# Four tiles instead of two for the decoded weights on their way to DRAM, two of them in the last operand of the attention

## The chip, the cores and the metric

The kernel runs on one core of one Trainium2 chip. The metric is the device time of one execution in microseconds (us), lower is better; the time given for a kernel is the median of its runs.

## The reference, cut to what matters

The program is an attention layer followed by two feed-forward layers, in float32 precision (every matrix product below is built from two parts of each operand, a high and a low one).

```python
# attention, per batch and head (4 x 8 heads, 576 rows, width 64)
scores = (q @ k.T) / 8 + minimum(-(cum_t - cum_s), 0), causal   # cum: running sum of max(s, 0)
x = softmax(scores) @ v                       # -> (4, 576, 512)
# first layer, per batch
h = maximum(x @ w_in, 0); u, v = h[..., :512], h[..., 512:]
v_s = w_spatial @ layernorm(v) + b_spatial
x = (u * v_s) @ w_out
# second layer
x_prev = x shifted by one row
xk = mu_k * x + (1 - mu_k) * x_prev;  xr = mu_r * x + (1 - mu_r) * x_prev
out = sigmoid(xr @ w_r) * (maximum(xk @ w_k, 0) ** 2 @ w_v)
```

All inputs arrive as 64-bit floats. The weight matrices are decoded in the kernel: each 128x256 block of 64-bit values becomes a float32 high part and a float32 low part.

## The kernel before, in words

**Decoding the weights.** The six weight matrices (`d_wv`, `d_wu` from `moe_w_in`, `d_wo`, `d_wk0`, `d_wk1`, `d_wr`, `d_w2`; lines 203 to 208) are cut into 64 jobs of 128x256 values. A job goes through five parts (lines 118 to 154):

- `dL` (line 120): a DMA on SyncE's (SP's) queue loads 256 KB into a tile `raw`, of which there are three (pool `stl`).
- `dF` (lines 128, 129): two ScalarE (ACT) instructions make `g` and a scaled low word from it.
- `dD` (lines 134, 136, 139): three VectorE (DVE) instructions, then one addition on GpSimd (POOL, line 141), give the float `f`.
- `dT` (lines 146 to 150): ACT copies `f`, rounded, into the first half of a tile `hl` (line 101), and POOL subtracts that from `f` into the second half (line 116). The pool `stg` gives two tiles `hl`, used in turn.
- `dS` (line 153): a DMA on SP's queue stores `hl` (256 KB) into the DRAM tensor of its matrix.

Each part takes the oldest job that the part before it has finished. `dec_step` (line 164) issues one of each, in the order `dS dT dD dF dL`, so a job moves on by one part per step and a load is used by `dF` two steps after it. Line numbers such as L101, L116 are those of shared helpers: on ACT L101 is only this copy; on POOL and DVE L116 is any two-part subtraction, told apart by the tile it writes.

**Order.** Nothing is scheduled by the compiler: every engine and the SP queue run their instructions in the order in which the program issues them. Up to the end of the attention, written-out lists (`START`, `ORDER`, `TAIL1`, `TAIL2`, lines 526 to 595 and 866 to 870) say where each decode part stands among the other work. After `TAIL2` comes the loop over the four batches `b` (lines 893 to 938). For each: `gate_u` (8 units, for b > 0, a decode step after every second one), `spatial` (8 units, a step after every second), `gate_v` of the next batch (4 or 5 units of 12 matmuls, a step after every second), `proj` (8 units, a step after every second). All these matmuls go to eight PSUM tiles used in turn. `tick()` (line 641) issues what was put off from the unit before.

**What gate_v needs.** During the first four `spatial` units the next batch's activations are split (`split_x`, lines 658 to 667): ACT copies the high part `XH` (line 659), and one tick later DVE subtracts it (L116, `big<-x`) to give the low part `XL`. Each `gate_v` unit begins with matmuls over `XH` and `XL` of parts 0 to 3 in this order (`three`, line 676; L682 in the profile).

**BIG.** The tile `BIG` (line 72) holds three groups of 5,120 float32 per partition. In the attention a group holds the four operands U, W, V, X of a pair of heads. Pair 15, the last one, uses group 0. After it, columns 0 to 4095 of group 0 hold the weight `WU`; group 1 holds `XH` and `XL`, group 2 the weight `WV`. Columns 4096 to 5119 of group 0, the end of X of pair 15, are used by nothing in the kernel before. The last matmuls that read X of pair 15 are those of `st_E(15)` (L440), issued in `TAIL1`.

Of the kernel before, what the change touches and what calls it, by code (L numbers as in the profile page):

```python
# [9 lines left out]
F32R = mybir.dt.float32r  # L10
# [15 lines left out]
def tile_kernel(  # L26
# [47 lines left out]
    def part_of(g, c0, n, w):  # L74
        return BIG[:, g].rearrange("p a b -> p (a b)")[:, c0:c0 + n * w].rearrange("p (n w) -> p n w", n=n)
# [7 lines left out]
    rctx = ctx.enter_context(ExitStack())  # L83

    def pool(c, name, bufs, space=None, **kw):
        if space is not None:
            kw["space"] = space
        return c.enter_context(tc.tile_pool(name=name, bufs=bufs, **kw))

    wdram = pool(rctx, "wdram", 1, bass.MemoryType.DRAM)  # L90
    stg = pool(rctx, "stg", 2, side="right")
    stl = pool(rctx, "stl", 3, side="right")
    WN = 256
    jobs, loaded, first = [], [], []
    n_done, last = [0], {}

# [18 lines left out]
    def subtract(eng, **kw):  # L115
        (nc.gpsimd if eng == "P" else nc.vector).tensor_tensor(op=ALU.subtract, **kw)  # L116

    def dec_load(j):
        t = stl.tile([128, WN], I64, tag="raw", name="raw")
        nc.sync.dma_start(out=t, in_=j[0])  # L120
        loaded.append((t,) + j[1:])

    def dec_first(t, *dst):
        w32 = t.bitcast(I32).rearrange("p (n t) -> p n t", t=2)
        low = t.bitcast(U32).rearrange("p (n t) -> p n t", t=2)[:, :, 0]
        top, topf = w32[:, :, 1], t.bitcast(F32).rearrange("p (n t) -> p n t", t=2)[:, :, 1]
        g = stg.tile([128, WN], F32, tag="g", name="g")
        nc.scalar.activation(out=g, in_=topf, func=ACTF.Abs)
# [3 lines left out]
    def dec_second(low, top, g, *dst):  # L132
# [4 lines left out]
            out=gi, in0=gi, scalar1=3, scalar2=0x3FFFFFFF, op0=ALU.logical_shift_left, op1=ALU.bitwise_and)  # L137
        f = stg.tile([128, WN], I32, tag="f", name="f")
        nc.vector.scalar_tensor_tensor(  # L139
# [4 lines left out]
    second, third = [], []  # L144

    def dec_third(f, dst):
        hl = stg.tile([128, 2, WN], F32R, tag="hl", name="hl")
        COPY[ENGINE["dH"]](hl[:, 0, :], f.bitcast(F32))
        subtract(ENGINE["dO"], out=hl[:, 1, :], in0=f.bitcast(F32), in1=hl[:, 0, :].bitcast(F32))
        third.append((hl, dst))  # L150

    def dec_store(hl, dst):
        nc.sync.dma_start(out=dst, in_=hl.bitcast(F32))
        n_done[0] += 1

    PARTS = {"dS": (third, dec_store, 0), "dT": (second, dec_third, 0), "dD": (first, dec_second, 0),
             "dF": (loaded, dec_first, 1), "dL": (jobs, lambda *j: dec_load(j), 0)}

# [10 lines left out]
    def weight(nm, src, c0, n):  # L169

        d = wdram.tile([128, 2, n, 512], F32, name=nm)
        for kc in range(n):
            for o in range(0, 512, WN):
                jobs.append((src[128 * kc:128 * kc + 128, c0 + o:c0 + o + WN], d[:, :, kc, o:o + WN]))
        last[nm] = len(jobs)
# [633 lines left out]
    def prep_b():  # L809
        b_lo = WS[1][96:97, 4, :]  # L810
        nc.scalar.copy(WS[1][64:65, 4, :], brow[64:65, :])
        nc.scalar.copy(b_lo, brow[96:97, :])
        nc.vector.tensor_tensor(out=b_lo, in0=brow[96:97, :], in1=b_lo.bitcast(F32), op=ALU.subtract)
# [69 lines left out]
    def prep_0():  # L883
        nc.gpsimd.memset(WS[1][64:128, 4, :].bitcast(F32), 0.0)
        prep_b()

    tail["B0"] = prep_0
    for nm in TAIL2.split():
        tail[nm]()
# [165 lines left out]
```

## Time and profile before

| | |
|---|---|
| three runs | 707.02, 708.51, 709.27 us (median 708.51) |
| the profiled execution | 707.71 us |
| its span, first to last instruction | 706.0 us |
| mean granted TensorE clock | 0.995 |
| busy: TensorE (PE), DVE, ACT, POOL | 677.7, 507.0, 374.3, 355.1 us |

The profile is one execution. Times of rows are us from the start of its span. PE is TensorE's matmuls, PEld its weight loads, SPq an instruction in SyncE's queue. In a timeline row, the text in brackets is how long the engine sat idle before that instruction and what ended the idle time. PEclk is the granted TensorE clock, 1.00 being 2.4 GHz and 0.50 being 1.2 GHz.

### The profile page before, as it was taken

How to read it: one execution, taken by the hardware profiler on the slowest of the kernel's cores; microseconds unless marked ns; L12 is line 12 of the kernel's file. 1: busy time of each engine (PE TensorE's matmuls, PEld its weight loads, DVE VectorE, ACT ScalarE, POOL GpSimd, SP SyncE). 2: the span in 40 equal slices, each digit the busy share in tenths (PEclk: the TensorE clock that was granted, in tenths of full speed). 3: DMA queues.
4: the chain of work that ended last, by engine and by line, in shares of the span. 5: the costliest groups of instructions: out<-in, count | busy, mean ns of one | idle time of the engine just before them, and what ended most of it. 6: DMA issues, size and time to landing. Idle time of an engine off the chain costs nothing.

```text
span 706.0 us, 11479 instructions
## 1 busy us (share of the span) xinstructions
PE 677.7 (96%) x3842; PEld 596.2 (84%) x3842; DVE 507.0 (72%) x1054; ACT 374.3 (53%) x840; POOL 355.1 (50%) x528
## 2 busy tenths in 40 slices
PE   4899999999999989999998999999999999999998
PEld 3687777778877789999998899998989889898987
DVE  8867677767762578857867858369788786968763
ACT  6678988989983475554555535341332414133230
POOL 4635656656566557446646637442434434244430
PEclk9999999999999999999999999999999999999999
DMA  8344645555447627454244466360001010000101
GB/s 180 95 107 126 163 120 154 134 138 151 118 112 233 210 84 220 135 170 129 93 144 154 141 210 205 107 285 16 31 0 46 1 45 2 16 31 0 45 1 45
DMA packets 100930, 77.61 MB, mean 110 GB/s; under 512 B 66949, under 2 KB 83749, under 8 KB 100359
## 3 DMA queue, kind: packets, MB, share of 16 engines
q1 hardware_dynamic: 98455, 76.28, 36.6%
q10 hardware_dynamic: 2416, 0.60, 0.4%
q8 instruction: 30, 0.49, 0.3%
q14 instruction: 29, 0.24, 0.1%
HBM read 54.05 MB, written 21.79 MB: 107 GB/s over the span
## 4 chain that ended last, share of the span: by engine, by line
PE 64%; DVE 10%; DMA 9%; ACT 8%; issue 3%; POOL 3%; SPq 2%; ACTq 0%; DVEq 0%; POOLq 0%
PE mm L682 43%; PE mm L767 5%; PE ps L440 4%; PE pv L487 4%; PE s L401 3%; DMA q<-in_q_dram 3%; DMA rd<-r 2%; ACT big L364 2%; PE pv L484 2%; PE t L347 2%; DMA r<-pt 2%; DMA d_wr<-hl 1%; DMA d_w<-hl 1%; DVE jk L408 1%; DVE big L369 1%
## 5 line engine op out<-in xcount | busy, mean ns | idle before, releaser
L682 PE MATMUL mm<-big 128*128 128x384 f32 (+2 forms) x1176 | 208.4, 336 | 6.3 <-ACT vr L719 3.0
L682 PEld LDWEIGHTS mm<-big 128*128 128x128 f32 x1176 | 193.7, 190 | 17.7 <-DVE big L116 4.0
L408 DVE CUSTOM_DVE_ANT_0 jk<-s,mask 128x288 bf16<-128x288 f32 (+4 forms) x160 | 64.3, 429 | 36.4 <-PE s L401 35.5
L682 PE MATMUL mm<-w,vb 128*128 128x512 f32 (+1 forms) x304 | 90.4, 381 | 0.0
L972 DVE TENSOR_TENSOR r<-r 128x384 f32<-128x384 f32 x48 | 53.7, 1119 | 46.6 <-ACT r L969 46.6
L440 PE MATMUL ps<-big 128*128 128x288 f32 (+4 forms) x384 | 84.5, 336 | 0.6
L401 PE MATMUL s<-big 128*128 128x448 f32 (+3 forms) x192 | 74.0, 427 | 7.7 <-DVE mx L408 3.6
L116 POOL TENSOR_TENSOR hl<-f,hl 128x256 fp32r<-128x256 f32 x64 | 50.6, 791 | 55.4 <-ACT hl L101 49.8
L460 ACT ACTIVATE e<-ps 128x288 f32<-128x288 f32 (+3 forms) x160 | 64.8, 435 | 21.7 <-PE ps L440 19.1
L141 POOL TENSOR_TENSOR f<-f,raw 128x256 int32<-128x256 int32 x64 | 51.6, 806 | 49.0 <-DVE f L139 23.0
L487 PE MATMUL pv<-e,vp 128*128 128x448 f32 (+3 forms) x256 | 73.7, 387 | 0.0
L440 PEld LDWEIGHTS ps<-big 128*128 128x128 f32 x384 | 61.7, 199 | 13.9 <-issue 7.2
L682 PEld LDWEIGHTS mm<-w,vb 128*128 128x128 f32 x304 | 56.0, 188 | 11.2
L401 PEld LDWEIGHTS s<-big 128*128 128x128 f32 x192 | 37.9, 206 | 30.1 <-DVE mx L408 23.8
L992 DVE RECIPROCAL rr<-rr 128x512 f32<-128x512 f32 x18 | 60.4, 3353 | 0.6
L515 POOL TENSOR_TENSOR x<-pt,rb 64x576 f32<-64x576 f32 x32 | 45.4, 1420 | 26.3 <-DMA rb<-rd 23.3
L464 POOL TENSOR_SCALAR_AFFINE_SELECT e<-e 128x128 f32<-128x128 f32 (+1 forms) x160 | 41.8, 287 | 30.0 <-ACT e L460 28.9
L767 PE MATMUL mm<-ws,vb 128*128 128x288 f32 x384 | 56.1, 295 | 0.0
L973 ACT CAST vb<-r 128x384 fp32r<-128x384 f32 x48 | 24.6, 513 | 56.9 <-DVE r L972 56.9
L767 PEld LDWEIGHTS mm<-ws,vb 128*128 128x128 f32 x384 | 52.6, 188 | 0.0
L682 PE MATMUL mm<-gh,wo 128*128 128x288 f32 x256 | 51.4, 295 | 0.0
L708 POOL TENSOR_TENSOR gh<-mix,vb 128x384 fp32r<-128x384 f32 x24 | 25.4, 1069 | 49.2 <-ACT vb L707 49.2
(129 smaller groups left out, 1329.6 us busy)
## 6 DMA issues: line engine op xcount, KB each, us to landing
rb<-rd SPq DMA_DIRECT2D x16, 288.0 KB
out_dram<-rr SPq DMA_DIRECT2D x17, 256.0 KB
q<-in_q_dram SPq DMA_DIRECT2D x32, 128.0 KB
raw<-in_moe_w_in_dram SPq DMA_DIRECT2D x16, 256.0 KB
vp<-in_v_dram SPq DMA_DIRECT2D x32, 128.0 KB
raw<-in_moe_w_k_dram SPq DMA_DIRECT2D x16, 256.0 KB
d_wk<-hl SPq DMA_DIRECT2D x16, 256.0 KB
raw<-in_moe_w_v_dram SPq DMA_DIRECT2D x16, 256.0 KB
```

The lines of the kernel that those rows point to most:

```text
L116: (nc.gpsimd if eng == "P" else nc.vector).tensor_tensor(op=ALU.subtract, **kw)
L141: nc.gpsimd.tensor_tensor(out=f, in0=f, in1=low, op=ALU.add)
L401: nc.tensor.matmul(out=ps[:, 0:kn], lhsT=W[g][:, h, 128 * i:128 * i + 128], rhs=X[g][:, h, k0:k0 + kn], start=True, stop=True,)
L408: nc.vector.tensor_tensor_reduce(out=jk[r0:128, 0:kn], in0=ps[r0:128, 0:kn], in1=mask[r0:128, m0:m0 + kn], scale=1.0, scalar=(dst if mid e ...
L440: nc.tensor.matmul(out=ps[:, o:o + b - a], lhsT=st[g][:, h, 128 * j:128 * j + 128], rhs=mv[g][:, h, 64 + a:64 + b], start=(n == 0), stop=( ...
L460: nc.scalar.activation(out=e[:, o:o + n], in_=ps[:, 0:n], func=ACTF.Exp)
L487: nc.tensor.matmul(out=pv[:, 1, 448 - w:448], lhsT=lt, rhs=e[:, OFF[j]:OFF[j] + w], start=False, stop=(j == 4),)
L515: (nc.gpsimd if ENGINE[f"n3{h}"] == "P" else nc.vector).tensor_tensor(out=X1[64 * h:64 * h + 64, hp, b, 1:S + 1], in0=hold["t"][0:64, h, : ...
L682: nc.tensor.matmul(out=ps, lhsT=x, rhs=y, start=(m == 0), stop=(m == n - 1))
L767: nc.tensor.matmul(out=o, lhsT=x[:, sc, dd], rhs=y[:, sc, t], start=(sc == 0 and m == 0), stop=False)
L972: nc.vector.tensor_tensor(out=r, in0=r, in1=r, op=ALU.mult)
L992: nc.vector.reciprocal(out=r, in_=r)
```

## The change

The two tiles `hl` are taken out of the pool `stg` and made two tiles of a pool of their own, kept in a list `ring` and used in turn. Before `TAIL2` two more tiles are appended to the list: views of columns 4096 to 4607 and 4608 to 5119 of group 0 of `BIG`. From there on four tiles are used in turn.

```diff
     stg = pool(rctx, "stg", 2, side="right")
     stl = pool(rctx, "stl", 3, side="right")
+    sth = pool(rctx, "sth", 1, side="right")
     WN = 256
+
+    ring = [sth.tile([128, 2, WN], F32R, name=f"hl{i}") for i in range(2)]
...
     def dec_third(f, dst):
-        hl = stg.tile([128, 2, WN], F32R, tag="hl", name="hl")
+        hl = ring.pop(0)
+        ring.append(hl)
         COPY[ENGINE["dH"]](hl[:, 0, :], f.bitcast(F32))
         subtract(ENGINE["dO"], out=hl[:, 1, :], in0=f.bitcast(F32), in1=hl[:, 0, :].bitcast(F32))
         third.append((hl, dst))
...
+    ring.extend(part_of(0, 4096 + 512 * i, 2, WN) for i in range(2))
     tail["B0"] = prep_0
     for nm in TAIL2.split():
         tail[nm]()
```

## Rows read from the trace of the kernel before

**Rows 1.** The page, part 1: busy us, share, instructions of TensorE.

```profile
PE 677.7 (96%) x3842; PEld 596.2 (84%) x3842; DVE 507.0 (72%) x1054; ACT 374.3 (53%) x840; POOL 355.1 (50%) x528
```

**Rows 2.** Waits of PE, 235 to 445 us, complete: us in total, times, longest.

```profile
PE mm L682 <- ACT vr L719: 3.0, 1, 3.0
PE mm L682 <- DVE big L116: 2.6, 3, 2.0
PE mm L682 <- ACT x L785: 0.4, 1, 0.4
PE mm L792 <- ACT ut L758: 0.2, 1, 0.2
```

**Rows 3.** Timeline of PE: gate_v of batches 1, 2, 3 (start, us, matmuls).

```profile
278.17 11.09 PE L682 MATMUL mm<-big 128*128 128x512 f32 x48
...
329.32 2.72 PE L682 MATMUL mm<-big 128*128 128x512 f32 x11
332.35 11.40 PE L682 MATMUL mm<-big 128*128 128x512 f32 x49 [0.31 <-DVE big L116]
...
383.81 2.02 PE L682 MATMUL mm<-big 128*128 128x512 f32 x8
...
387.79 0.96 PE L682 MATMUL mm<-big 128*128 128x512 f32 x3 [1.96 <-DVE big L116]
...
389.06 10.28 PE L682 MATMUL mm<-big 128*128 128x512 f32 x37 [0.32 <-DVE big L116]
```

**Rows 4.** Windows, PE alone: length, busy us (matmuls), PEclk, DMA share, GB/s.

```profile
390.00:391.00 1.00, 1.00 (x4) 0.50 0.09 30
```

**Rows 5.** Timeline of DVE: three of batch 3's four XL subtractions.

```profile
380.79 0.74 DVE L116 TENSOR_TENSOR big<-x,big 128x576 fp32r<-128x576 f32 x1
...
386.59 1.14 DVE L116 TENSOR_TENSOR big<-x,big 128x576 fp32r<-128x576 f32 x1
...
388.02 0.99 DVE L116 TENSOR_TENSOR big<-x,big 128x576 fp32r<-128x576 f32 x1
```

**Rows 6.** Waits of ACT, whole span, those on the stores of `hl`.

```profile
ACT hl L101 <- DMA d_wk<-hl: 15.4, 9, 2.9
...
ACT hl L101 <- DMA d_w<-hl: 12.8, 6, 5.8
...
ACT hl L101 <- DMA d_wr<-hl: 7.9, 6, 2.6
```

**Rows 7.** Timeline of ACT: copies into `hl`, the first two are seven steps apart.

```profile
359.55 0.41 ACT L101 CAST hl<-f 128x256 fp32r<-128x256 f32 x1 [1.54 <-POOL f L141]
...
380.80 0.41 ACT L101 CAST hl<-f 128x256 fp32r<-128x256 f32 x1 [1.42 <-DMA d_w<-hl]
...
416.54 0.41 ACT L101 CAST hl<-f 128x256 fp32r<-128x256 f32 x1 [5.79 <-DMA d_w<-hl]
```

**Rows 8.** The chain that ended last, 361 to 372 us: start, us, what.

```profile
361.99 4.04 DMA d_wr<-hl
...
366.61 0.74 POOL hl L116
367.34 0.76 POOL f L141
...
368.12 0.34 SPq L120
...
368.55 2.88 DMA d_wr<-hl
```

**Rows 9.** Timeline of DVE: one step's part of the decoding.

```profile
369.95 0.60 DVE L134 TENSOR_SCALAR g<-g 128x256 f32<-128x256 f32 x1 [1.19 <-ACT g L128]
370.59 0.73 DVE L136 TENSOR_SCALAR g<-g 128x256 int32<-128x256 int32 x1
371.41 0.43 DVE L139 SCALAR_TENSOR_TENSOR f<-raw,g 128x256 int32<-128x256 int32 x1
```

**Rows 10.** Instructions on the tile `hl`, 250 to 440 us: count, duration ns, starts.

```profile
L101 ACT CAST hl<-f x44: 399/407/412, 257.2 to 432.9; 128x256 fp32r<-128x256 f32 x44
```

## The prediction

> **What bounds the kernel now.** I read the page's busy times first: TensorE is busy for 677.7 of the 706.0 us [rows 1]. Where one engine is that full, only its holes can be won, so the next view is the list of PE's waits over the stretch in which the four tiles exist, from the start of `TAIL2` to the end of the decoding. It is short and complete [rows 2]: 3.0 us on ACT's line 719, 2.6 us on DVE's line 116, 0.4 us on ACT's line 785, 0.2 us on ACT's line 758. The wait on line 719 ends before the first copy into `hl` that `TAIL2` issues (257.2 us, [rows 10]), since it belongs to the last `gate_v` units of batch 0 that `TAIL1` issues. The change can't reach it. The other three can be reached.
>
> The timeline of PE places the 2.6 us [rows 3]. They lie in `gate_v`: 0.31 us at 332 us and 1.96 and 0.32 us at 388 and 389 us, each time on a subtraction `big<-x`, which is `XL`. So PE has run out of everything else and waits for the low part of the next batch's activations. The hole costs more than its idle time: the same 48 matmuls take 11.09 us in `gate_v` of batch 1 and, for batch 3, run from 383.81 to 389.06 + 10.28 = 399.34 us, which is 15.53 us. The difference is 4.44 us, of which 2.28 are idle. The other 2.16 us are the clock: after the hole the granted clock is 0.50, that is 1.2 GHz, where it was 2.4 GHz [rows 4].
>
> Why is `XL` late? The waits of ACT say it: before the copy into `hl` ACT waits 15.4 + 12.8 + 7.9 = 36.1 us, 21 times, for the stores of `hl` [rows 6]. ACT runs in order, so its copy of `XH` (line 659) stands behind those waits, and DVE's `XL` behind `XH`. The chain view shows the loop that sets this pace [rows 8]: POOL finishes a tile and the addition behind it (0.74 and 0.76 us), that frees a `raw` tile, SP issues the load it had been stuck on (0.34 us), and only then the store that stands behind the load; the store takes 2.88 or 4.04 us, and ACT may then write that tile again. With two tiles this loop closes every second step.
>
> **The change part by part.** *Tiles of their own in place of the pool's two, before `TAIL2`.* The same two tiles, in the same order, as many instructions; the copy still waits for the store of two steps earlier. None of the waits in rows 6 lies in the attention's stores (`d_wv`, `d_wu`), so nothing is hidden there that could appear. Zero; its cover is that no instruction is added. Should the tracked waits differ by a semaphore instruction, I bound that at some hundredths of a us, each way, beside other work.
>
> *Two more tiles from `TAIL2` on.* No DMA, ACT or POOL instruction is added or moved; 44 copies [rows 10] go to four tiles in place of two. Their first use has to wait for the last reader of X of pair 15, a matmul that `TAIL1` issued long before. From then on a copy waits for the store of four steps earlier, issued three steps before. A store in the loop above lands within two steps, so these waits should go.
>
> *What is late next.* With the stores gone, the decoding's next loop is that of the three `raw` tiles, closed every third step: SP's issue 0.34 us, the load's landing, an ACT pass of about 0.41 us, DVE's three (0.60 + 0.73 + 0.43 = 1.76 us, [rows 9]), POOL's addition 0.76 us. The landing of a load has no row here; the nearest rows are the stores of the same 256 KB, 2.88 and 4.04 us, and I keep both ends. That is 6.2 to 7.3 us for three steps, 2.1 to 2.4 us a step. Now a step takes (380.80 - 359.55) / 7 = 3.04 us [rows 7]. Over those seven steps ACT gains 4.2 to 6.8 us, so `XH` and `XL` of batch 3 come earlier by that much, as far as PE's own `spatial` results allow.
>
> *What is enough.* PE needs the third `XL` at 383.81 + 2.02 = 385.83 us and gets it at 386.59 + 1.14 = 387.73; it needs the fourth three matmuls later (3 x 11.09 / 48 = 0.69 us), at 386.5, and gets it at 388.02 + 0.99 = 389.01 [rows 3, 5]. So 2.5 us earlier closes the hole, and the slower end of the estimate gives 4.2. At 2.7 us a step it would just be closed. The same holds one batch before, where the hole is 0.31 us and ACT waits for `d_wk` even longer.
>
> *The sum.* Batch 3's `gate_v`: 4.44 us, idle and clock. Batch 2's `gate_v`: from 329.32 to 343.75 is 14.43 us for 60 matmuls, against 60 x 11.09 / 48 = 13.86, so 0.57 us [rows 3]. The wait on line 785: 0.38 us at most; it is a copy of `proj` that stood behind ACT's longest wait on a store, 5.79 us [rows 7], and that goes too: 0.4 us. Line 758's 0.2 us lies in `TAIL2` before any wait on a store; nothing. Together 5.4 us. After 440 us the decoding is over and PE has no hole until the last units of the output, so what is won is kept: every fetch of a weight stands behind PE's own reading of the buffer and moves with it. The profiled execution takes 707.71 us, its span and 1.7 around it; less 5.4 that is 702.3. The median of the runs shown is 0.8 above that execution, so the forecast is 703.1 us.
>
> **The rivals.** *The loads take the stores' place.* If a load landed only after some 5 us, the loop over `raw` would take 8.3 us for three steps, 2.8 a step, and ACT would wait on line 128 as it now does on line 101. For it: SP issues load and store back to back, and faster steps put more of them on the queues. Against it: the two landings shown are below that. The hole of batch 3 would shrink by perhaps half a microsecond and the clock would fall all the same: 708 us. Chance 0.11.
>
> *DVE and POOL get in each other's way.* The same subtraction `XL` takes 0.74, 1.14 and 0.99 us [rows 5], longer where POOL is at work. If ACT's waits had been keeping the two apart, DVE would now lose that on most of its work, 0.4 us on each operation with two operands in SBUF. Some six of these stand between the first `spatial` result and the fourth `XL`, so 2.4 us would come off the 4.2 to 6.8 gained, at the lower end 1.8 would be left of the 2.5 needed, and a hole of 0.7 us with the fall of the clock behind it would cost 0.7 + 2.16 = 2.9 of the 4.44: 706.0 us. Against it: most of that stretch already runs at the longer times. Chance 0.06. The Trainium skill, "SBUF — State Buffer", section "Who interferes with whom", speaks for this rival: it says that a DVE instruction with two SBUF inputs contends with a GpSimd instruction that reads SBUF, and that the loser is blocked for the whole instruction. By that rule alone a blocked `XL` could lose up to a POOL pass, 0.74 us, and the trace's 0.25 to 0.40 agrees in direction.
>
> *Slower: the new tiles are taken for the whole of BIG.* If the waits were derived for `BIG` as one object, each matmul that reads any of it would wait for the last write into the two new tiles. Half of the 44 steps write there; PE would wait for at least the copy and the subtraction, 0.41 + 0.74 us, 22 times: 25 us more, 734 us. It decides from the first step that writes such a tile with PE behind it. Against it: DVE's and ACT's writes of `XL` and of `mix`, and the fetches into WU and WV, go into other parts of `BIG` beside matmuls that read it, and PE's complete list of waits names no transfer [rows 2]. Chance 0.05.
>
> *It doesn't do what it says* would be four tiles whose waits stay, since a store is issued late rather than landing late. But SP lets one store pass per step, so never more than two are open; it would look like the first rival, 708 us, and is in its chance.
>
> **How the numbers follow.** Forecast 0.78, loads 0.11, contention 0.06, slower 0.05. A measurement of this kernel tells about 0.3%, 2.1 us, from no change: faster is below 706.4. The forecast's own range is 701.5 (the runs shown reach 1.5 below their median) to 704.7 (the holes of batch 2 and line 785 stay, and 0.6 of the rest). To hold the time 8 times in 10 the range goes on to 706.9, over the contention case; no change and slower are left out. Faster: the forecast and part of the contention case, 0.80. Same: the rest of it and the loads, 0.15. Slower 0.05.
>
> **What would show it right or wrong.** Right: no wait of ACT's line 101 on a store after 257 us, or a few tenths in all; what is left there is on POOL's line 141; PE without idle between 320 and 440 us of its span, clock 1.00 throughout; the 48 matmuls of batch 3's `gate_v` in 11.1 us; the 3.0 us on line 719 unchanged. Wrong: ACT waiting for `raw` at line 128; `XL` still ending later than PE needs it; any wait of PE on `hl`; or a new hole after 440 us that gives the gain back.

## The result: 6.2 us faster, and the profile after

| | before, on the same chip | after |
|---|---|---|
| median (range) | 707.76 us (706.56 to 709.27), 4 runs | 701.29 us (700.02 to 701.61), 4 runs |
| ratio after/before, 95% interval | | 0.9912 [0.9893, 0.9931] |
| the profiled execution, its span | 707.71, 706.0 us | 700.02, 698.3 us |

The ratio is worked out from all the runs of both kernels and is not the quotient of the two medians; it is 6.2 us of 707.76, between 4.9 and 7.6. The forecast was 5.4 us and 703.1 us: faster, as predicted. The median is 1.8 us below the forecast and 0.2 us below 701.5, the low edge of its range. Part of that is the kernel before, which ran faster here than in the three runs that the forecast started from: set against their 708.51 us the ratio gives 0.9912 x 708.51 = 702.3 us, inside the range. In the lines of the changed kernel most numbers are three to five higher: L101, L116, L120, L141 are now L104, L119, L123, L144, and L682, L719, L758, L785 are now L686, L723, L762, L789. Half of the decoded tiles lie in `BIG`, so a tile `hl` shows as `big` in two steps of four.

Part 1 of the page of the changed kernel, beside [rows 1]: PE is busy 5.1 us less with the same 3842 matmuls.

```profile
PE 672.6 (96%) x3842; PEld 592.2 (85%) x3842; DVE 497.9 (71%) x1054; ACT 376.8 (54%) x840; POOL 355.8 (51%) x528
```

The waits of PE from 235 to 445 us, complete, beside [rows 2]. Nothing of the wait on DVE's subtraction and nothing of the wait on the copy of `proj` is left. The wait on line 723 stands (2.6 for 3.0 us). The waits on line 762 have grown from 0.2 to 1.3 us; the section on the hardware says where they come from.

```profile
PE mm L686 <- ACT vr L723: 2.6, 1, 2.6
PE mm L686 <- ACT ut L762: 1.1, 2, 0.9
PE mm L796 <- ACT ut L762: 0.2, 1, 0.2
```

The timeline of PE in the changed kernel: `gate_v` of batches 1, 2 and 3, beside [rows 3], and last the `gate_u` of batch 3. Each is one stretch without a bracket, that is without idle time. Batch 3's 48 matmuls take 11.09 us as batch 1's do, where they took 15.53; batch 2's 60 take 13.81 in place of 14.43.

```profile
276.52 11.09 PE L686 MATMUL mm<-big 128*128 128x512 f32 x48
...
327.67 13.81 PE L686 MATMUL mm<-big 128*128 128x512 f32 x60
...
381.54 11.09 PE L686 MATMUL mm<-big 128*128 128x512 f32 x48
...
405.12 12.88 PE L686 MATMUL mm<-big 128*128 128x288 f32 x96
```

The waits of ACT in the changed kernel, 245 to 440 us, beside [rows 6]: 36.1 us on stores are gone without a rest, and over the whole span too no copy waits for a store. What ACT now waits for in the decoding is POOL's addition and the loads: 6.7 + 5.0 + 1.4 = 13.1 us on `raw`.

```profile
ACT g L131 <- DMA raw<-in_moe_w_v_dram: 6.7, 4, 2.9
ACT g L131 <- DMA raw<-in_moe_w_k_dram: 5.0, 5, 2.6
ACT hl L104 <- POOL f L144: 4.7, 6, 1.3
...
ACT big L104 <- POOL f L144: 3.4, 5, 1.5
...
ACT g L131 <- DMA raw<-in_moe_w_r_dram: 1.4, 2, 0.9
```

The timeline of ACT in the changed kernel, copies of steps one, six and eight of the same stretch as [rows 7]. From the first to the sixth are five steps in 11.79 us, 2.36 us each; all seven take 370.14 - 352.27 = 17.87 us, 2.55 each, where [rows 7] had 21.25 and 3.04. The last two steps are slower, 3.04 us each: by then ACT has caught up and waits for PE's results (1.19 us on line 762 ahead of the seventh copy).

```profile
352.27 0.41 ACT L104 CAST big<-f 128x256 fp32r<-128x256 f32 x1 [1.53 <-POOL f L144]
...
364.06 0.41 ACT L104 CAST hl<-f 128x256 fp32r<-128x256 f32 x1
...
370.14 0.40 ACT L104 CAST big<-f 128x256 fp32r<-128x256 f32 x1
```

**Where the time went.** The last long piece of the chain of waits gives a mark behind the decoding. In the changed kernel it is the following line, and it ends at 695.08 us, 313.54 us after batch 3's `gate_v` began.

```profile
432.84 262.24 PE mm L686 x1344
```

In the kernel before the same piece ends at 702.80, 318.99 us after that `gate_v` began at 383.81: 5.45 us were lost behind that point. With the 0.62 of batch 2's `gate_v` it is 6.07 us. The two spans differ by 7.7. The other 1.6 us lie before the two added tiles can act: the hole on line 719 began at 246.07 us before and on line 723 at 244.73 after, and part of the difference is the price of that hole. That this part varies from execution to execution is shown by other executions: in experiment 2, with the same attention, this hole ends at 252.36 us, in the changed kernel at 247.36, and in the kernel before at 249.03 in the one profile and 247.22 in the other.

### The profile page after: what moved, and what is told of

Read it like the earlier page. It is cut to its first block, busy times and chain, and to the rows that moved or that the text cites. A ratio compares the mean times of both kernels' runs of the same rounds, so it can differ in the third digit from the quotient of the medians.

```text
span 698.3 us, 11475 instructions
## 1 busy us (share of the span) xinstructions
PE 672.6 (96%) x3842; PEld 592.2 (85%) x3842; DVE 497.9 (71%) x1054; ACT 376.8 (54%) x840; POOL 355.8 (51%) x528
## 4 chain that ended last, share of the span: by engine, by line
PE 76%; DMA 7%; ACT 6%; DVE 4%; SPq 2%; issue 2%; POOL 1%; ACTq 0%; DVEq 0%; POOLq 0%
PE mm L686 54%; PE mm L771 7%; PE ps L444 3%; PE pv L491 3%; DMA q<-in_q_dram 3%; PE s L405 2%; DMA rd<-r 2%; ACT big L368 2%; PE pv L488 2%; PE t L351 2%; DVE jk L412 1%; DMA r<-pt 1%; SPq L256 1%; DVE big L373 1%; ACT e L464 1%
## 5 line engine op out<-in xcount | busy, mean ns | idle before, releaser
L686 PE MATMUL mm<-big 128*128 128x384 f32 (+2 forms) x1176 | 204.3, 332 | 3.8 <-ACT vr L723 2.6
L686 PEld LDWEIGHTS mm<-big 128*128 128x128 f32 x1176 | 191.4, 188 | 13.3 <-ACT vr L723 2.9
L686 PE MATMUL mm<-w,vb 128*128 128x512 f32 (+1 forms) x304 | 90.4, 381 | 0.0
L144 POOL TENSOR_TENSOR f<-f,raw 128x256 int32<-128x256 int32 x64 | 51.8, 809 | 48.6 <-DVE f L142 22.7
L444 PEld LDWEIGHTS ps<-big 128*128 128x128 f32 x384 | 60.1, 194 | 14.5 <-issue 7.4
L686 PEld LDWEIGHTS mm<-w,vb 128*128 128x128 f32 x304 | 56.0, 188 | 11.2
L686 PE MATMUL mm<-gh,wo 128*128 128x288 f32 x256 | 51.3, 294 | 0.0
L712 POOL TENSOR_TENSOR big<-mix,big 128x384 fp32r<-128x384 f32 x24 | 25.7, 1074 | 47.4 <-ACT big L711 38.7
```

Source lines behind the costliest of these rows:

```text
L144: nc.gpsimd.tensor_tensor(out=f, in0=f, in1=low, op=ALU.add)
L444: nc.tensor.matmul(out=ps[:, o:o + b - a], lhsT=st[g][:, h, 128 * j:128 * j + 128], rhs=mv[g][:, h, 64 + a:64 + b], start=(n == 0), stop=( ...
L686: nc.tensor.matmul(out=ps, lhsT=x, rhs=y, start=(m == 0), stop=(m == n - 1))
L712: nc.gpsimd.tensor_tensor(out=dst[1][:, kc, :], in0=t, in1=dst[0][:, kc, :].bitcast(F32), op=ALU.subtract)
```

## Experiments

The theory was the prediction's: two tiles make ACT wait for stores, those delay `XH` and `XL`, and PE's hole in batch 3 goes when the steps run faster. Its rivals: something else in the change does it (own tiles, their place), or the gain lies in the attention. All kernels are edits of the changed kernel unless it says otherwise. Each ratio is to runs of the kernel before made beside that experiment; their median was 708.07 us for experiments 1 to 4, 706.66 for 5 to 8 and 706.45 for 9 to 11.

**1. The own tiles without the two in `BIG`.**

```diff
-    ring.extend(part_of(0, 4096 + 512 * i, 2, WN) for i in range(2))
```

> The two tiles of the ring alone, without the two in BIG: the part of the change that touches the attention. Theory (the whole gain is the waits on stores after the attention): the same time as before, within 1 us, with the 36 us of ACT's waits on stores back, and batch 3's 48 matmuls of gate_v from first to last in about 15.5 us. Rival (tiles outside the pool, or their place in memory, help the attention too, since the changed kernel stood 1.65 us earlier already when spatial's first operand was transposed): 1.5 us or so faster than before, with the hole still there.

Measured: 709.5 us, ratio to before 1.0022 [0.9996, 1.0047], which does not tell it from before (the median is 1.4 us higher, where "within 1 us" was expected). The gain is gone entirely, so it comes from the two added tiles and not from the new pool. The waits of ACT of this kernel, 245 to 440 us, have the stores again, 34.9 us:

```profile
ACT hl L104 <- DMA d_wk<-hl: 13.8, 9, 2.6
...
ACT hl L104 <- DMA d_w<-hl: 12.5, 6, 5.7
...
ACT hl L104 <- DMA d_wr<-hl: 8.6, 4, 3.7
```

Its timeline of PE in batch 3's `gate_v` has the hole at the same two places, but shorter and without the slow matmuls behind it: 13.29 us to the end of the last, not the expected 15.5.

```profile
388.27 2.02 PE L686 MATMUL mm<-big 128*128 128x512 f32 x8
391.59 0.98 PE L686 MATMUL mm<-big 128*128 128x512 f32 x3 [1.29 <-DVE big L119]
392.87 8.69 PE L686 MATMUL mm<-big 128*128 128x512 f32 x37 [0.30 <-DVE big L119]
```

Part of what wasn't lost here was lost a little later, on the copy of `proj`. Its PE timeline:

```profile
421.71 3.44 PE L686 MATMUL mm<-big 128*128 128x288 f32 x24 [1.14 <-ACT x L789]
425.70 3.44 PE L686 MATMUL mm<-big 128*128 128x288 f32 x24 [0.55 <-ACT x L789]
```

and its ACT timeline just before: the copy of a decoded tile waits 5.75 us for a store, and the `proj` copies that PE is waiting for stand behind it.

```profile
420.32 0.40 ACT L104 CAST hl<-f 128x256 fp32r<-128x256 f32 x1 [5.75 <-DMA d_w<-hl]
421.28 0.68 ACT L789 COPY x<-mm 128x288 f32<-128x288 f32 x2
```

**2. Three tiles.**

```diff
-    ring.extend(part_of(0, 4096 + 512 * i, 2, WN) for i in range(2))
+    ring.extend(part_of(0, 4096 + 512 * i, 2, WN) for i in range(1))
```

> One tile in BIG in place of two, three in turn. Theory: the loop over the store then closes every third step; copy, subtraction, addition, SP's issue and landing (0.41 + 0.74 + 0.76 + 0.34 + 2.9 to 4.0) are 5.1 to 6.3 us for three steps, 1.7 to 2.1 a step, which is below the 2.1 to 2.4 of the loop over the three tiles of raw. So the time of the changed kernel, within 0.7 us, and at most some 4 us of ACT's waits on stores, none of them before PE's hole. Rival (the fourth tile is what does it): 2 us or more slower than the changed kernel, with a hole in batch 3's gate_v.

Measured: 702.28 us, 0.9918 [0.9894, 0.9943], all of the gain within the interval. `gate_v` takes 13.81 and 11.09 us. Two waits of ACT on stores are left, of 3.1 and 2.4 us, both on stores into `d_w`. That is 5.5 us where at most some 4 were expected, and the median is 1.0 us above the changed kernel's where at most 0.7 was expected; the intervals do not tell the two apart. The fourth tile saves these 5.5 us of ACT, and PE doesn't feel them: its waits from 235 to 445 us are those of the changed kernel within 0.1 us.

**3 and 4. Two tiles in one part of the decoding, four in the rest.** The list keeps four tiles, and `width` says how many are in turn. In experiment 3 it is 2 from `proj` of batch 1 to `spatial` of batch 2 and 4 elsewhere after `TAIL1`; in experiment 4 the two numbers are exchanged.

```diff
+    width = [2]
...
         hl = ring.pop(0)
-        ring.append(hl)
+        ring.insert(width[0] - 1, hl)
...
+    width[0] = 4
...
+            if b == 2:
+                width[0] = 4
...
+        if b == 1:
+            width[0] = 2
```

> Four tiles, but only two of them in turn from the proj of batch 1 to the spatial of batch 2, the stretch whose waits stand before the large hole. Theory that the lag is inherited: with four tiles up to there ACT enters this stretch some 5 us less behind PE; at 3.04 us a step the fourth XL would be ready about 2 us before PE needs it, so no hole: the time of the changed kernel, within 1 us, though some 9 us of waits on stores come back. Rival (the lag is made inside this stretch): the hole of 2.3 us and the fall of the clock come back, 4.4 us slower than the changed kernel.

> The reverse: two tiles in turn all along, four only from the proj of batch 1 to the spatial of batch 2. ACT enters the stretch as late as in the kernel before; at 2.1 to 2.4 us a step it gains 4 to 6 us, more than the 2.5 that close the hole. Theory: batch 3's gate_v in 11.1 us, 4.4 us gained; batch 2's gate_v keeps its 0.6, so 2 us or so slower than the changed kernel at most, and 4.4 to 5.5 us faster than before. If the lag can't be made good inside this stretch: a hole stays and the gain is below 3 us.

Measured: experiment 3, 702.03 us, 0.9924 [0.9897, 0.995]; experiment 4, 704.06 us, 0.9944 [0.9922, 0.9967]. In experiment 3 ACT waits for stores again in just the stretch ahead of batch 3's `gate_v`, six times and 7.9 us for those into `d_wr`. Seven steps take 378.04 - 357.32 = 20.72 us, 2.96 each, nearly the old pace, and still there is no hole: its 48 matmuls take 11.09 us from 386.56 on. The reason stands in its DVE timeline (helper lines are one higher again here), the fourth `XL`, which ends at 385.76 us, before that `gate_v` begins.

```profile
384.82 0.94 DVE L120 TENSOR_TENSOR big<-x,big 128x576 fp32r<-128x576 f32 x1
```

So the lateness in batch 3 was a debt that ACT had run up over the batches before; one slow batch alone doesn't make it. In experiment 4 the debt of the batches before is paid back in one fast stretch (2.37 us a step, (376.17 - 359.55) / 7): batch 3's `gate_v` takes 11.09 us, batch 2's has its loss back (14.27 us). It is 4.0 us faster than before, a little less than the 4.4 to 5.5 expected. So four tiles on either side suffice to close the large hole; those outside the stretch bring the whole gain within the interval, and those inside it alone leave batch 2's loss.

**5. The kernel before, with the store ahead of the load.** Two tiles, nothing in `BIG`. In a step, `dT` goes ahead of `dS`, so a store is issued in the step in which its tile is written, right behind the subtraction, and in SP's queue ahead of that step's load and not behind the one that waits for `raw`.

```diff
-    PARTS = {"dS": (third, dec_store, 0), "dT": (second, dec_third, 0), "dD": (first, dec_second, 0),
+    PARTS = {"dT": (second, dec_third, 0), "dS": (third, dec_store, 0), "dD": (first, dec_second, 0),
```

> The kernel before with its two tiles, and one thing moved: in each decode step of the loop over the batches the store stands right behind the subtraction of its own step, ahead of that step's load, in place of at the head of the next step, behind that load. Theory (the loop runs over SP's queue, where the store was stuck behind a load that waits for raw): the loop becomes copy, subtraction and landing, 0.41 + 0.74 + 2.9 to 4.0 = 4.1 to 5.2 us for two steps, 2.0 to 2.6 a step, which is under the 2.7 that closes the hole of batch 3. So most of the gain without any new tile: 701.5 to 703.5 us, with some 10 us of ACT's waits on stores left. Rival (SP's order is not part of the loop, only the number of tiles is): 707 to 708 us, the hole as before.

Measured: 701.78 us, 0.9921 [0.9898, 0.9944]. An exchange of two entries brings what the two tiles brought. The timeline of PE:

```profile
328.59 13.81 PE L682 MATMUL mm<-big 128*128 128x512 f32 x60
...
382.46 11.09 PE L682 MATMUL mm<-big 128*128 128x512 f32 x48
```

The waits of ACT on stores, whole span, 5.7 us where [rows 6] had 36.1:

```profile
ACT hl L101 <- DMA d_w<-hl: 4.7, 2, 2.4
...
ACT hl L101 <- DMA d_wr<-hl: 1.0, 2, 0.8
```

The waits of SP's queue show why. In the kernel before:

```profile
SPq L120 <- POOL f L141: 110.3, 38, 6.7
...
SPq L153 <- POOL hl L116: 24.6, 10, 7.0
```

and in this one:

```profile
SPq L153 <- POOL hl L116: 103.9, 44, 7.0
...
SPq L120 <- POOL f L141: 16.7, 21, 3.2
```

SP now stands waiting at the store, which leaves the moment its tile is ready; before, it stood at the load, and a store whose tile was ready stood behind it. In [rows 8] the subtraction ends at 366.61 + 0.74 = 367.35 us and the store is issued at 368.55, 1.2 us later. In this kernel's timelines of POOL, of SP's queue and of ACT the same gap is 0.02 us, and the copy that next takes this tile starts 4.2 us after the issue:

```profile
355.72 0.75 POOL L116 TENSOR_TENSOR hl<-f,hl 128x256 fp32r<-128x256 f32 x1 [0.52 <-ACT hl L101]
...
356.49 0.52 SPq L153 DMA_DIRECT2D d_wr<-hl  x1
...
360.71 0.41 ACT L101 CAST hl<-f 128x256 fp32r<-128x256 f32 x1 [0.83 <-DMA d_wr<-hl]
```

So this store did not land faster than the 2.88 and 4.04 us of [rows 8]. The stores were late in being issued, as the chain of [rows 8] had it, and two tiles are enough when they are not.

**6. The same order on the changed kernel**, the same exchange.

> The changed kernel with the same move of the store. Theory: with four tiles no copy waits for a store before PE needs anything, so the time of the changed kernel within 0.7 us. If it is faster by more, something of the store's lateness still cost time there.

Measured: 701.24 us, 0.9920 [0.9894, 0.9945]. The two remedies don't add up; after either one there is no wait of PE left for them to remove.

**7 to 9. The hole that the change can't reach.** The 2.6 us on line 723 remain. Three attempts: `g4` issued ahead of `g3c` at the end of `TAIL1`; the tile `UT` allocated ahead of `WS`, in the thought that its place made line 762 wait for POOL's last rows (line 519); and a new end of `TAIL1` that puts decoding parts behind POOL's rows.

```diff
-               ... dF vn31 dD dF g3c g4 wn31 g2c dT wn30"""
+               ... dF vn31 dD dF g4 g3c wn31 g2c dT wn30"""
```

> The changed kernel, and in the first of the two lists at the end of the attention the last gate_v unit of batch 0 (g4) put ahead of the normalisation of the unit before (g3c), so that ACT's copy out of PSUM at line 723 no longer stands behind a copy that waits for DVE. The changed kernel still has PE idle there for 2.6 us, then 0.2 and 0.9. Theory: the 2.6 us go, and PE stops a little later at the copies of line 762, which wait until 250.6 us for POOL's last normalised rows; so 0.5 to 2.5 us faster than the changed kernel, and more if the clock no longer falls. Rival: the hole only moves to line 762 and grows there by as much: the same time.

```diff
-    WS = [bc.tile([128, NC, S], F32R, name=f"ws{i}") for i in range(2)]
     UT = bc.tile([128, 4, S], F32, name="ut")
+    WS = [bc.tile([128, NC, S], F32R, name=f"ws{i}") for i in range(2)]
```

> The changed kernel with the tile UT placed first in its pool, ahead of the spatial weights, so that it lies over other buffers of the attention. Theory: ACT's wait of 2.5 us at line 762 for POOL's last normalised rows is one for memory, and goes; the two holes of 0.2 and 0.9 us behind it shrink, 0.5 to 1.5 us faster than the changed kernel. Rival: the spatial weights now take the wait (line 802 stands right behind on ACT), the same time.

```diff
-               ... dF vn31 dD dF g3c g4 wn31 g2c dT wn30"""
+               ... dF vn31 dF g4 g3c wn31 g2c wn30 dT dD"""
```

> The changed kernel with the end of the first list rearranged: the last gate_v unit of batch 0 ahead of the normalisation of the unit before, and POOL's two decode instructions (the addition, 0.8 us, and the subtraction into the tile, 0.7 us) behind POOL's last normalised rows in place of ahead of them. ACT's line 762 waits for these rows until 250.6 us. Theory: they are ready up to 1.5 us earlier and the hole that moved to line 762 shrinks from 3.3 to about 1.8 us: 699.8 us, 1 to 1.5 us faster than the changed kernel. Rival: the rows wait for their transfer, not for POOL, and the time is that of the changed kernel.

Measured: 701.27 us, 0.9935 [0.9909, 0.9961]; 701.48 us, 0.9926 [0.9895, 0.9958]; 702.58 us, 0.9935 [0.9901, 0.9968]. None is better than the changed kernel. In the first PE's one wait between 235 and 445 us is now 3.3 us on line 762: the hole has moved to the next line of ACT. In the second line 762 waits for line 519 as before (2.4 us), so this other place of `UT` doesn't free it; why it waits stays open. In the third POOL itself runs out of work, since its rows on line 519 wait up to 1.30 us for their transfer.

**10 and 11. Both kernels once more, unedited**, to see how much of the two profiles is one execution's chance.

> The changed kernel once more, unedited, for more runs beside those of the kernel before and a second profile. Theory: a ratio of 0.989 to 0.993, gate_v of batches 2 and 3 without idle, no wait of ACT on a store after 257 us. What the second profile is for: whether the granted clock falls after the hole of some 2.6 us at the end of the attention, which the change does not touch; in the first profile it did not, in the kernel before it did, over a hole of about the same length.

> The kernel before once more, unedited, for a second profile of its holes. Theory: gate_v of batch 3 has a hole of 1.3 to 2.3 us again, on the low part of the activations. Whether the clock falls behind it is open: it did in the first profile, and did not in the kernel with two tiles of their own. Without the fall PE should come to gate_u of batch 3 earlier and wait there longer, 1 to 2 us in place of 0.4, on line 785, so that the stretch from gate_v of batch 3 to the last proj takes 55.5 to 56.5 us either way (51.3 in the changed kernel).

Measured: the changed kernel 701.26 us, 0.9930 [0.9903, 0.9957], `gate_v` 13.81 and 11.09 us again, and 380.12 to 431.43 + 262.24 = 693.67 us, 313.55 after 313.54. The kernel before, one execution of 704.7 us; its timeline of PE:

```profile
327.48 2.72 PE L682 MATMUL mm<-big 128*128 128x512 f32 x11
330.46 11.42 PE L682 MATMUL mm<-big 128*128 128x512 f32 x49 [0.27 <-DVE big L116]
...
381.94 2.02 PE L682 MATMUL mm<-big 128*128 128x512 f32 x8
...
384.99 0.97 PE L682 MATMUL mm<-big 128*128 128x512 f32 x3 [1.03 <-DVE big L116]
...
386.27 8.68 PE L682 MATMUL mm<-big 128*128 128x512 f32 x37 [0.31 <-DVE big L116]
...
414.85 3.44 PE L682 MATMUL mm<-big 128*128 128x288 f32 x24 [0.89 <-ACT x L785]
...
419.05 3.45 PE L682 MATMUL mm<-big 128*128 128x288 f32 x24 [0.76 <-ACT x L785]
```

A window of PE of this execution behind the hole (length, busy us and matmuls, PEclk, DMA share, GB/s): 1.00, where [rows 4] had 0.50.

```profile
387.00:388.00 1.00, 1.00 (x7) 1.00 0.14 48
```

The waits on line 785 are 1.65 us together, as expected without the fall of the clock. From the start of `gate_v` to the last `proj` it is 437.34 - 381.94 = 55.40 us, 0.1 short of the range expected (440.20 - 383.81 = 56.39 in the first profile). Its long piece of the chain ends at 437.34 + 262.45 = 699.79 us, 317.85 after its `gate_v` began at 381.94.

## Why the prediction was right, and the terms it mis-sized

**The mechanism** held at each step. The copies' waits on stores are gone (36.1 us to none), the step is shorter, `XL` is in time, PE has no hole between 320 and 440 us, and taking the two tiles away (experiment 1) or making the stores early without them (experiment 5) undoes or replaces the whole. How ACT's wait reaches `XL` stands in the DVE timeline of the kernel before, the second subtraction of batch 3, which [rows 5] leaves out:

```profile
382.81 1.41 DVE L116 TENSOR_TENSOR big<-x,big 128x576 fp32r<-128x576 f32 x1 [0.91 <-ACT big L659]
```

The copy of `hl` at 380.80 us waited for a store [rows 7], the copy of `XH` stands behind it, and DVE waits for that copy. The third `XL`, the one that PE waits for, comes 2.4 us later still, because DVE's part of a decode step stands in between.

**The pace.** Forecast 2.1 to 2.4 us a step from the loop over `raw`, 2.36 measured over five steps, the slow end. The next loop is the one named: 13.1 us of ACT's waits are on loads. But *"Over those seven steps ACT gains 4.2 to 6.8 us"* is mis-sized: the seven steps gained 21.25 - 17.87 = 3.4 us, because ACT caught up with PE after five. More had been gained before: measured against the start of batch 3's `gate_v`, the first of these copies comes 383.81 - 359.55 = 24.3 us ahead in the kernel before and 381.54 - 352.27 = 29.3 us ahead in the changed one, 5.0 us earlier. That is the debt of experiment 3, and the prediction had no term for it.

**What is enough.** 2.5 us of advance were wanted, 4.2 to 6.8 forecast. In the changed kernel PE begins `gate_v` at 381.54 and needs the fourth `XL` 2.7 us later, at 384.2 (2.02 and 0.69, as the prediction counted); it ends at 378.86, 5.4 us early, where it had been 2.5 us late: an advance of 7.9 us on PE, more than forecast, for the reason just given. In the DVE timeline of the changed kernel, beside [rows 5]:

```profile
371.13 0.93 DVE L119 TENSOR_TENSOR big<-x,big 128x576 fp32r<-128x576 f32 x1
...
372.87 1.18 DVE L119 TENSOR_TENSOR big<-x,big 128x576 fp32r<-128x576 f32 x1
...
376.42 1.15 DVE L119 TENSOR_TENSOR big<-x,big 128x576 fp32r<-128x576 f32 x1
...
377.87 0.99 DVE L119 TENSOR_TENSOR big<-x,big 128x576 fp32r<-128x576 f32 x1
```

**The sum: 5.4 forecast, 6.07, 4.90 and 4.79 measured.** The loss that the change removes can be read in three executions with two tiles, each against the changed kernel's 313.54 and 13.81 us:

| | behind the start of batch 3's `gate_v` | batch 2's `gate_v` | together |
|---|---|---|---|
| the profile of before | 318.99 - 313.54 = 5.45 | 0.62 | 6.07 |
| before once more | 317.85 - 313.54 = 4.31 | 0.59 | 4.90 |
| experiment 1 | 318.33 - 313.54 = 4.79 | 0 | 4.79 |

The forecast lies between them, which is in part luck: two of its terms were wrongly taken as fixed, and it has no term for 0.6 us of the first row. The step *"The other 2.16 us are the clock"* is the first. In the kernel before once more the three pieces of that `gate_v` take 2.02 + 0.97 + 8.68 = 11.67 us at a clock of 1.00, 0.58 more than 11.09: that much goes at the two breaks of the stream beside the idle time shown. So of the 2.16 only about 10.28 - 8.68 = 1.6 was the clock, in that one execution, and in the two others none. The step *"The wait on line 785: 0.38 us at most"* is the second. Where the clock stays up, PE reaches `gate_u` of batch 3 earlier, while the copies of `proj` still stand behind the same waits of ACT for stores, the longest over 5 us, and waits there 0.89 + 0.76 = 1.65 us, and in experiment 1 1.14 + 0.55 = 1.69. The two terms hang together: beside the first profile the loss in `gate_v` is 2.5 us smaller in before once more (13.01 us in place of 15.53) and 2.2 us smaller in experiment 1, and the wait on line 785 is 1.3 us longer in both. So about half of what PE doesn't lose at `XL` or to the clock it loses at line 785. Summed, the forecast for both was 4.44 + 0.38 = 4.82 of the 5.45; the remaining 0.6 us lies further on, of which 0.36 in the last long piece (262.60 against 262.24), and I had no term for it.

**The median.** 701.29 is 1.8 us under the forecast. Of that 0.75 is the base: before ran at 707.76 beside it, not 708.51. The other 1.1 is the measured difference of medians, 6.5 us, over the forecast 5.4, and the interval of 4.9 to 7.6 doesn't tell 5.4 from the 6.07 of the profile. The second set of runs (experiment 10) gave 0.9930, which is 4.9 us of 706.45, below the forecast.

**The rivals.** *The loads take the stores' place*: they do, as ACT's next wait, but at 2.36 us a step and not 2.8, which costs PE nothing. Whether a fourth tile `raw` would shorten the step was not tried, and PE has no hole there to win. *DVE and POOL in each other's way*: the four subtractions take 0.93 + 1.18 + 1.15 + 0.99 = 4.25 us; in the profile of before 0.74 + 1.41 + 1.14 + 0.99 = 4.28, the second of them the row above. The first is 0.19 longer, the sum is not, so the rival doesn't decide here; it wasn't tried by itself. *The new tiles taken for the whole of `BIG`*: PE's complete waits name no copy or subtraction of `hl` or its parts in `BIG`. *It doesn't do what it says*: the argument against it was that SP lets one store pass per step. Experiment 5 shows that SP's order was a larger part of the loop than that sentence made it: the stores were issued late, and more tiles covered the delay rather than removed it. Nor were 2.88 and 4.04 us the longest landings: the store ahead of the wait on line 785 took 6.78 us in the kernel before, in the chain view, and SP's queue had issued a piece of the fetch of `d_wk` right ahead of it, from 412.37 us on. That the fetch made it slow is not shown. Both waits on `d_w` that experiment 5 leaves lie behind the same fetch.

```profile
413.64 6.78 DMA d_w<-hl
```

## What to carry to other kernels

How many buffers a ring needs was decided here by the loop that closes over it, and the in-order DMA queue was part of that loop: ahead of a deeper ring, see what the queue stands waiting at, for here an exchange of two issues (store ahead of the load) brought as much as two tiles of memory, and three tiles as much as four. The hole of the bounding engine was the sum of a helper's lateness over many steps, and either of two stretches that let the helper catch up closed it. Price such holes together: about half of what was not lost at one wait for the late engine was lost at the next, so the sum of the two (4.8, 3.6 and 3.9 us in three executions) was steadier than the larger term (4.4, 1.9 and 2.2).

## What the runs showed of the hardware

The granted clock doesn't answer a hole in the same way each time. At the end of the attention PE stands idle on line 719 or 723 (724 in experiments 3 and 4) for some 2.3 to 3.1 us in every execution but those of experiments 7 and 9. After 2.63 us in the changed kernel, 2.66 in the kernel before once more and 2.63 in experiment 2 the clock stayed at 1.00 (2.4 GHz), as it did after 2.28 in experiment 3, 2.29 in the changed kernel once more and 2.42 in experiment 1. After 2.51 in experiment 6, 2.56 in experiment 4 and 2.39 in experiment 5 it fell to 0.50 (1.2 GHz), as it did after 2.96 in the profile of before and 3.10 in experiment 8. So the holes with a fall run from 2.39 to 3.10 us and those without one from 2.28 to 2.66: the length of the hole alone doesn't decide, and what does stays open. PE's timeline of experiment 6, and two windows of it:

```profile
248.41 8.22 PE L686 MATMUL mm<-big 128*128 128x288 f32 x48 [2.51 <-ACT vr L723]
```

```profile
248.00:249.00 1.00, 0.59 (x2) 0.57 0.15 50
249.00:250.00 1.00, 1.00 (x6) 0.50 0.73 242
```

and the same places of the changed kernel:

```profile
247.36 3.46 PE L686 MATMUL mm<-big 128*128 128x288 f32 x24 [2.63 <-ACT vr L723]
251.06 1.86 PE L686 MATMUL mm<-big 128*128 128x288 f32 x12 [0.24 <-ACT ut L762]
253.81 1.85 PE L686 MATMUL mm<-big 128*128 128x288 f32 x12 [0.89 <-ACT ut L762]
```

```profile
248.00:249.00 1.00, 1.00 (x10) 1.00 0.69 227
```

At the high clock the 24 matmuls and the two times 12 behind them are broken by waits of 0.24 and 0.89 us on line 762; at the low clock the 48 run as one stretch, and there is no wait in them. From the start of the 48 to their end it is 253.81 + 1.85 - 247.36 = 8.30 us in the one and 8.22 in the other: here the next wait has taken the whole price of the fall. It isn't always so even: the same 48 matmuls took 9.29 us in experiment 5, with the fall and a wait of 0.86 us on line 758 in it, and 9.48 in experiment 1 without a fall, where the waits on line 762 were 1.42 and 0.89 us. In `gate_v` of batch 3, the clock fell after idle times of 1.96 and 0.32 us in the profile of before, and not after 1.03 and 0.31 or 1.29 and 0.30 in the two other executions with two tiles.
